# First k and q by head over two queues, a later second part, and last rows in four blocks: sliding-window attention before a gated FFN

## The chip, the cores and the metric

The kernel runs on one core of a Trainium2 chip. The metric is device microseconds of one execution, from the first to the last instruction of the launch. A profile of one execution has a span that is a little shorter than that run's time (323.3 against 324.98 us before the change).

## The reference

Attention with a causal window of 64 tokens, then a feed-forward layer with a ReLU gate. Only shapes and the computation are kept:

```python
B, H, S, D = 8, 8, 576, 64                      # q, k, v: (B, H, S, D) float32
rel = pos[:, None] - pos[None, :]
mask = (rel >= 0) & (rel < 64)
scores = where(mask, q @ k.T / sqrt(D), -1e9)
attn = softmax(scores)                          # per head
x = (attn @ v).transpose(0, 2, 1, 3).reshape(4608, 512)
out = (relu(x @ w_gate) * (x @ w_val)) @ w_out  # w_gate, w_val: (512, 1536), w_out: (1536, 512)
```

## The kernel before

The 4608 rows of x are cut into token tiles: four of 384 and six of 512. Attention works on units of 192 tokens; a unit covers all eight heads, and two units make a tile of 384. With 576 tokens per batch, units 0, 1 and 2 are the tokens 0 to 191, 192 to 383 and 384 to 575 of batch 0. Heads are taken in two halves of four, `hh` 0 for heads 0 to 3 and `hh` 1 for heads 4 to 7; within a half, head g lies in partitions 32g to 32g+31.

k and q come from HBM with 32 runs of tokens per head, one run in each partition, 18 tokens long. A vector-engine transpose of 32x32 blocks (`qk_trans`, L185) turns them to the layout that the score matmuls need. Everything after batch 0's first heads is loaded by GpSimd's DMA queue with a cast to fp16 on the way (`qk_load`, L167). Heads 0 to 3 of batch 0 are different: `first_load` (L172) takes all 576 tokens as fp32 over SP's queue, k and then q, and `first_round` (L178) rounds each to fp16 in two halves, one on the vector engine (DVE) and one on the scalar engine (ACT).

A unit then goes through these steps. `u_st` (L233) makes the scores on TensorE (PE), `u_exp` (L267) their exponentials on ACT, `u_mask` (L272) the mask on DVE (units 0 and 1 have the mask as a bias in the scores instead, `bias_mm`, L210), `u_pv` (L293) the values with a column of row sums, `u_recip` and `u_norm` (L307 to L317) the division, and `u_turn` (L327) transposes the result into the tile's `xt`. `v_load` (L191) brings v by GpSimd's queue, and `v_spread` (L200, L202) copies it to the other partition half, so that a window's 128 keys stand in one column of partitions.

`hidden` (L468) multiplies a tile's `xt` by wg and wv, block by block of the 12 blocks of 128 hidden columns; ACT applies the ReLU (L453) and DVE the gate (L456). `output` (L482) multiplies by wo, ACT copies PSUM to `o_sb` (L489), and SP stores it (L490). `output_last` (L505) treats the last 128 rows of the last tile on its own: two halves of 256 columns, and the second half is evacuated in two parts on two engines.

The weights come by `w_load` (L148, L150), four blocks of columns at a time, each of wg and wv in two transfers (the two halves of the contraction), also over GpSimd's queue and with a cast. They are issued behind k, q and v of the first units, so that the order on this queue is: k and q of heads 4 to 7, v of units 0 and 1, wg and wv 0 to 3, wg and wv 4 to 7, v of unit 2, wg and wv 8 to 11, then batch 1 and wo. `bands` (L100) makes the mask and the identity matrix on GpSimd, behind the first two loads.

The order of instructions on each engine is written out in the program. From the first `hidden` on, a planner (`Weaver`) keeps a modelled clock of PE's work and a heap of pieces with due times: `W.at(26.0, ...)` puts the scores of unit 2 behind the matmul group at which the modelled clock passes 26.0, and so on. The due times decide places in the engines' queues, not moments on the chip. `heat` issues matmuls of zeros ahead of the real work. The tile framework adds the semaphore waits; a DMA's completion is counted on one of eight semaphores in turn for each kind of queue, and a new DMA on a semaphore waits for the one before it there.

Of the kernel before, what the change touches and what calls it, by code (L numbers as in the profile page):

```python
# [10 lines left out]
FP32 = mybir.dt.float32  # L11
FP16 = mybir.dt.float16
# [32 lines left out]
def kernel(  # L45
# [10 lines left out]
    nc = tc.nc  # L56
    B, H, S, D = q.shape
    DM = H * D
# [7 lines left out]
    G = 4  # L66
# [3 lines left out]
    NS = 4  # L70
# [26 lines left out]
    bias = consts.tile([128, 64], FP16)  # L97
    ident = consts.tile([128, 128], FP16)

    def bands():  # L100


        nc.gpsimd.memset(mask, 1.0)
        nc.gpsimd.memset(ident, 1.0)
        for band, lo, hi in ((ident, 0, 0), (mask, 64, -1)):
            n = band.shape[1]
            nc.gpsimd.affine_select(  # L107
                out=band, in_=band, compare_op=mybir.AluOpType.is_ge, fill=0.0,
                base=lo, pattern=[[1, n]], channel_multiplier=-1,
            )  # L110
            nc.gpsimd.affine_select(
                out=band, in_=band, compare_op=mybir.AluOpType.is_ge, fill=0.0,
                base=hi, pattern=[[-1, n]], channel_multiplier=1,
            )

    def band_bias():

# [45 lines left out]
    def qk_load(b, name, hh):  # L163

        tile_ = nat[b, name, hh] = a_in.tile([128, S // 32 * D], FP16, name=f"{name}{hh}", bufs=2)
        src = (q if name == "q" else k)[b, G * hh:G * hh + G]
        nc.gpsimd.dma_start(tile_, src.rearrange("h (i j) d -> (h i) (j d)", i=32))  # L167

    def first_load(name):

        t32 = nat["32", name] = x_sb.tile([128, S // 32 * D], FP32, name=f"{name}32", bufs=1)
        nc.sync.dma_start(t32, (q if name == "q" else k)[0, 0:G].rearrange("h (i j) d -> (h i) (j d)", i=32))  # L172

    def first_round(name, copies):
        n = S // 32 * D // len(copies)
        to = nat[0, name, 0] = a_in.tile([128, S // 32 * D], FP16, name=f"{name}0", bufs=2)
        for i, copy in enumerate(copies):
            copy(to[:, n * i:n * i + n], nat["32", name][:, n * i:n * i + n])  # L178

    def qk_trans(b, name, hh, j0=0, j1=S // 32):  # L180

        src = nat[b, name, hh].bitcast(FP32).rearrange("p (j e) -> p j e", e=32)
        dst = qTs[b % 2][:, hh] if name == "q" else kTs[b % 2][:, hh, 64:64 + S]
        dst = dst.bitcast(FP32).rearrange("p c o -> p (c o)")
        nc.vector.transpose(dst.rearrange("p (i j) -> p j i", i=32)[:, j0:j1], src[:, j0:j1])  # L185
# [8 lines left out]
    def v_spread(u, copy=None, h0=0, h1=H):  # L194

        b, uu = divmod(u, UB)
        t = v16s[b % 2]
        copy = copy or nc.vector.tensor_copy
        for g0, g1 in (((0, 3),), ((4, 5),), ((6, 7),))[uu]:
            copy(t[64:128, g0:g1:2, h0:h1, 0:64], t[0:64, g0 + 1:g1 + 1:2, h0:h1, 0:64])  # L200
        for g0, g1 in (((2, 3),), ((4, 5),), ((6, 9),))[uu]:
            copy(t[0:64, g0:g1:2, h0:h1, 0:64], t[64:128, g0 - 1:g1 - 1:2, h0:h1, 0:64])  # L202
# [73 lines left out]
    def u_pv(u, hhs=(0, 1), banks=None):  # L276

        d = units[u]
        if "pv" not in d:
            if banks:  # L280
                d["pv"] = [one_bank("pv") for _ in range(2)]
            else:
                both = two_banks("pv")
                d["pv"] = [both[:, hh] for hh in range(2)]
                d["both"] = both
        for hh in hhs:
            to = d["pv"][hh]
            for w in range(UB):
                b, vw = divmod(UB * u + w, NG)
                for s in range(2):  # L290
                    for j in range(G):
                        c = VW * (2 * w + s)
                        nc.tensor.matmul(  # L293
                            to[32 * j:32 * j + 32, c:c + D + 1], p_of(u, G * hh + j, w)[:, 32 * s:32 * s + 32],
                            v16s[b % 2][:, vw, G * hh + j, 0:D + 1],
                            start=True, stop=True, skip_group_check=True)
        return 0.27 * len(hhs)
# [185 lines left out]
                         start=(f == 0), stop=(f == NF - 1))  # L483
        W.clock += 519 / 2400.0

    def out_evac(t, op, sub):
        def evac():
            o_sb = f_sb.tile([128, DM], FP32, name="o_sb")
            nc.scalar.copy(o_sb, op)  # L489
            nc.sync.dma_start(out[bass.ds(starts[t] + sub * 128, 128)], o_sb)  # L490
        W.at(W.clock, evac)

    def op_tile():
# [2 lines left out]
    def output(t, subs=None):  # L496
        for sub in range(widths[t] // 128) if subs is None else subs:
            op = op_tile()
            for f in range(NF):
                if f % 4 == 0:  # L500
                    W.advance(W.clock)
                out_mm(t, op, sub, f)
            out_evac(t, op, sub)

    def output_last(t):  # L505

        last = widths[t] // 128 - 1
        output(t, range(last))
        W.drain()
        for col in range(2):  # L510
            op = op_tile()
            for f in range(NF):
                g_sb, _ = gs[t]
                nc.tensor.matmul(op[:, 0:256], g_sb[:, f, bass.ds(last * 128, 128)], wo[:, f, 256 * col:256 * col + 256],
                                 start=(f == 0), stop=(f == NF - 1))
            parts = ((0, 256, nc.scalar.copy, nc.sync),) if col == 0 else (
                (0, 128, nc.scalar.copy, nc.scalar), (128, 256, nc.vector.tensor_copy, nc.sync))
            for c0, c1, copy, queue in parts:
                o_sb = f_sb.tile([128, DM], FP32, name="o_sb")
                copy(o_sb[:, c0:c1], op[:, c0:c1])  # L520
                queue.dma_start(out[bass.ds(starts[t] + last * 128, 128), 256 * col + c0:256 * col + c1], o_sb[:, c0:c1])

    def output_by_rows(t):
        ops = [op_tile() for _ in range(TT // 128)]
# [8 lines left out]
    with tc.manual_schedule():  # L533
        G3, V3, O3 = ([(wt, src, f0, f0 + 4) for f0 in (0, 4, 8)]
                      for wt, src in ((wg, moe_w_gate), (wv, moe_w_val), (wo, moe_w_out)))
        act, dve, pool = nc.scalar.copy, nc.vector.tensor_copy, nc.gpsimd.tensor_copy
        for name in "kq":
            first_load(name)
        for name in "kq":
            qk_load(0, name, 1)  # L540
        warm = consts.tile([128, 2], FP32)
        nc.vector.memset(warm, 0.0)
        nc.scalar.activation(warm[:, 1:2], warm[:, 0:1], ACT.Exp)
# [3 lines left out]
        nc.vector.memset(zero, 0.0)  # L547
        st_tiles(0)
        heat(6, units[0]["st"][3])
        bands()  # L550
        v_load(0, ((1, 0, 128), (3, 0, 64)))
        v_load(1, ((3, 64, 128), (5, 0, 128)))
        w_load(*G3[0], 15.2)
# [1 line left out]
        k_zeros()  # L555
        band_bias()

        first_round("k", (dve, act))
        u_bias(0)
        u_bias(1)  # L560
        qk_trans(0, "k", 0)
        first_round("q", (act, dve))
        qk_trans(0, "q", 0)
        for name in "kq":
            qk_trans(0, name, 1)
        for hh in range(2):
# [4 lines left out]
        for hh in range(2):  # L571
            v_spread(0, dve, G * hh, G * hh + G)
            u_pv(0, (hh,), True)
        v_spread(1, pool)
        for hh in range(2):
            u_recip(0, (hh,))
# [11 lines left out]
        v_load(2)  # L588
        w_load(*G3[2], 27.0)
        w_load(*V3[2], 29.6)  # L590
        W.at(26.0, lambda: u_st(2))
        plan_exps(26.0, 2)
        W.at(25.5, lambda: v_spread(2))
        plan_values(29.5, 2)

        for name in "kq":
            for hh in range(2):
# [106 lines left out]
```

The softmax here doesn't subtract the row's maximum and nothing guards it: scores larger than these inputs give would overflow.

## Time and profile before

| what | value |
|---|---|
| time, median of 3 runs | 324.99 us (324.95 to 325.98) |
| span of the profiled execution | 323.3 us (its run: 324.98) |
| mean granted TensorE clock | 0.989 |
| GpSimd's DMA queue | 18.29 MB written, 48.4% of 16 engines' span |
| SP's DMA queue | 10.55 MB, 8.9% |
| HBM | 37.75 MB read, 9.44 MB written |

The page lists busy times of the engines (PE is TensorE, PEld its weight loads, DVE VectorE, ACT ScalarE, POOL GpSimd, SP the queue of stores), then the chain of work that ended last. In a timeline, each line has the start, the busy time, engine, source line, operation, what it writes and reads, how many instructions are merged in it, and in brackets how long the engine had been idle and what ended that. Names with a q (SPq, ACTq, DVEq) are the engine's sequencer: it issues DMAs and waits for semaphores. Sizes on the page count the type that is written, so a cast load of 256 KB reads 512 KB.

### The profile page before, as it was taken

The numbers are of one execution on the slowest core, as the hardware profiler recorded it, in microseconds if no ns is written. First come the engines' busy times: TensorE is split into PE (matmuls) and PEld (weight loads), VectorE is DVE, ScalarE is ACT, GpSimd is POOL, SyncE is SP. The second block draws the span as 40 slices with busy tenths as digits, with TensorE's granted clock in tenths as the row PEclk, the third lists the DMA queues.
The fourth block names the chain that finished last, engine by engine and source line by source line (L and its number), as shares of the span: only waits on it lengthen the run. The fifth ranks groups of instructions, "written<-read, shape, count | busy, mean of one in ns | idle before, by whom it ended". The sixth has DMA issues, their size and how long they took to land.

```text
span 323.3 us, 8901 instructions
## 1 busy us (share of the span) xinstructions
PE 313.7 (97%) x3851; PEld 168.4 (52%) x3851; DVE 192.1 (59%) x370; ACT 127.0 (39%) x249; POOL 93.7 (29%) x138
## 2 busy tenths in 40 slices
PE   5699999999999999999999999999999999999995
PEld 2586958656556644454445444454445444544443
DVE  5947962687938749564755656674767146723410
ACT  3444324534424523532454234613372237223321
POOL 8766335285900390029000910071000000000000
PEclk9599999999999999999999999999999999999999
DMA  7999998989590269019900892091001200020002
GB/s 215 186 196 210 194 107 174 155 150 163 83 211 4 15 108 181 3 12 124 214 5 2 111 203 24 2 122 70 0 2 38 97 0 2 21 111 3 0 34 98
DMA packets 52488, 29.48 MB, mean 91 GB/s; under 512 B 38880, under 2 KB 43872, under 8 KB 52448
## 3 DMA queue, kind: packets, MB, share of 16 engines
q0 software_dynamic: 46688, 18.29, 48.4%
q1 hardware_dynamic: 5616, 10.55, 8.9%
q8 instruction: 30, 0.49, 0.6%
q10 hardware_dynamic: 144, 0.07, 0.1%
q14 instruction: 10, 0.08, 0.1%
HBM read 37.75 MB, written 9.44 MB: 146 GB/s over the span
## 4 chain that ended last, share of the span: by engine, by line
PE 94%; DMA 2%; POOL 2%; issue 0%; ACT 0%; DVE 0%; DVEq 0%; POOLq 0%
PE h L468 59%; PE op L482 28%; PE st L233 3%; PE pv L371 2%; DMA v<-in_v_dram 2%; PE pv L293 1%; POOL v L191 1%; DMA out_dram<-o_sb 1%; POOL k L167 0%; POOL v L200 0%; POOL v L202 0%; ACT o_sb L489 0%; POOL q L167 0%; PE st L207 0%; POOL ident L107 0%
## 5 line engine op out<-in xcount | busy, mean ns | idle before, releaser
L456 DVE TENSOR_TENSOR g_sb<-r_sb,h 128x512 f16<-128x512 f32 (+1 forms) x120 | 75.4, 631 | 86.3 <-PE h L468 84.5
L468 PE MATMUL h<-xt,wg 128*128 128x512 f16 (+2 forms) x544 | 112.5, 338 | 0.1
L468 PE MATMUL h<-xt,wv 128*128 128x512 f16 (+2 forms) x544 | 111.3, 335 | 0.0
L453 ACT ACTIVATE r_sb<-h 128x512 f32<-128x512 f32 (+1 forms) x120 | 66.7, 558 | 89.5 <-PE h L468 80.4
L482 PE MATMUL op<-wo,g_sb 128*128 128x512 f16 x420 | 93.9, 379 | 0.0
L468 PEld LDWEIGHTS <-wg 128*128 128x128 f16 x544 | 51.5, 99 | 42.8 <-issue 0.5
L468 PEld LDWEIGHTS <-wv 128*128 128x128 f16 x544 | 50.5, 98 | 40.8
L482 PEld LDWEIGHTS <-g_sb 128*128 128x128 f16 x420 | 40.3, 98 | 47.1
L191 POOL DMA_DIRECT2D v<-in_v_dram x41 | 34.5, 861 | 95.0 <-PE pv L371 90.1
L489 ACT COPY o_sb<-op 128x512 f32<-128x512 f32 x35 | 20.5, 586 | 84.7 <-PE op L482 84.5
L356 DVE TENSOR_TENSOR pw<-pw,mask 128x512 f16<-128x512 f16 x48 | 19.3, 422 | 14.6 <-ACT pw L352 14.3
L352 ACT ACTIVATE pw<-st 128x512 f16<-128x512 f32 x48 | 25.7, 605 | 5.0 <-PE st L233 4.5
L200 POOL COPY v<-v 64x512 f16<-64x512 f16 (+1 forms) x21 | 15.5, 736 | 24.3 <-DMA v<-in_v_dram 23.4
L185 DVE STREAM_TRANSPOSE kT<-k 128x576 f32<-128x576 f32 x16 | 19.9, 1245 | 0.2 <-ACT k L178 0.2
L185 DVE STREAM_TRANSPOSE qT<-q 128x576 f32<-128x576 f32 x16 | 19.3, 1237 | 0.1
L267 ACT ACTIVATE p<-st 128x384 f16<-128x384 f32 (+1 forms) x40 | 14.0, 441 | 8.2 <-PE st L233 8.2
L391 DVE TENSOR_TENSOR xw<-pv,rw 128x448 f16<-128x448 f32 (+1 forms) x36 | 16.2, 507 | 0.4
L233 PE MATMUL st<-qT,kT 32*128 32x64 f16 x1152 | 12.9, 192 | 3.5 <-DVE qT L185 3.5
L202 POOL COPY v<-v 64x512 f16<-64x512 f16 (+1 forms) x21 | 15.9, 759 | 1.0
L233 PEld LDWEIGHTS <-kT 32*128 32x128 f16 x1152 | 10.8, 94 | 10.5 <-issue 8.5
L396 DVE STREAM_TRANSPOSE xt<-xw 128x1024 f16<-128x1024 f16 x12 | 14.9, 1244 | 0.4
L272 DVE TENSOR_TENSOR p<-p,mask 128x384 f16<-128x384 f16 x24 | 9.5, 414 | 3.6 <-ACT p L267 3.5
(46 smaller groups left out, 97.9 us busy)
## 6 DMA issues: line engine op xcount, KB each, us to landing
out_dram<-o_sb SPq DMA_DIRECT2D x35, 256.0 KB, 2.8
k<-in_k_dram POOLq DMA_DIRECT2D x15, 288.0 KB, 5.7
q<-in_q_dram POOLq DMA_DIRECT2D x15, 288.0 KB, 8.6
v<-in_v_dram POOLq DMA_DIRECT2D x31, 128.0 KB, 8.9
wg<-in_moe_w_gate_dram POOLq DMA_DIRECT2D x6, 256.0 KB, 6.4
wv<-in_moe_w_val_dram POOLq DMA_DIRECT2D x6, 256.0 KB, 7.7
wo<-in_moe_w_out_dram POOLq DMA_DIRECT2D x3, 512.0 KB, 12.2
v<-in_v_dram POOLq DMA_DIRECT2D x10, 64.0 KB, 5.8
```

What stands on the lines that cost most here:

```text
L185: nc.vector.transpose(dst.rearrange("p (i j) -> p j i", i=32)[:, j0:j1], src[:, j0:j1])
L191: nc.gpsimd.dma_start(v16s[b % 2][lo:hi, g, :, 0:64], v[b, :, 64 * g - 64 + lo:64 * g - 64 + hi].rearrange("h p d -> p h d"))
L202: copy(t[0:64, g0:g1:2, h0:h1, 0:64], t[64:128, g0 - 1:g1 - 1:2, h0:h1, 0:64])
L233: return [lambda dh=dh: nc.tensor.matmul(to, kTs[b % 2][rows, hh, 64 * w:64 * w + 128, dh], qTs[b % 2][rows, hh, 64 * w:64 * w + 64, dh], ...
L352: nc.scalar.activation(d["p"][g].rearrange("p n c -> p (n c)"), d["st"][g], ACT.Exp, scale=scale)
L356: nc.vector.tensor_tensor(p, p, mask[:, None, :].to_broadcast([128, 2 * QW, 64]), MUL)
L391: nc.vector.tensor_tensor(d["x"][:, hh, s0:s1], pv[:, :, 0:D].rearrange("p s (c e) -> p s e c", e=2), d["r"][:, hh, s0:s1, :, None].to_bro ...
L453: nc.scalar.activation(part(r_sb), part(h1), ACT.Relu)
L456: nc.vector.tensor_tensor(g_sb[:, f:f + w, c0:c0 + n], part(r_sb), part(h2), MUL)
L468: nc.tensor.matmul(h[:, b * n:b * n + n], wt[:, c, (f + b) * 128:(f + b) * 128 + 128], xt[:, c, c0:c0 + n], start=(c == 0), stop=(c == NC ...
L482: nc.tensor.matmul(op, g_sb[:, f, bass.ds(sub * 128, 128)], wo[:, f], start=(f == 0), stop=(f == NF - 1))
L489: nc.scalar.copy(o_sb, op)
```

## The change

Four things change together.

First, k and q of heads 0 to 3 of batch 0 are loaded in two parts: tokens 0 to 383, which units 0 and 1 use, and tokens 384 to 575, which only unit 2 uses. The first part of k goes out over SP's queue and that of q over ACT's queue, each as four transfers, one for each head (32 partitions). The second parts go over SP's queue; a one-column memset of their tiles on DVE, placed behind the v copies of unit 0, holds them back until then. Rounding and transposing are split in the same way, and the second part's is planned at due times 22.4 to 23.6.

Second, GpSimd makes the mask ahead of the load of k of heads 4 to 7, and the identity between that and the load of q.

Third, the due times of unit 2's work are 0.5 earlier.

Fourth, the last 128 rows are made in four blocks of 128 columns, each with its own tile, copied by ACT; three are stored by SP and the last one by ACT. The first rows of the last tile are stored in two transfers.

```diff
-        for band, lo, hi in ((ident, 0, 0), (mask, 64, -1)):
...
+    def band(to, lo, hi):
+        nc.gpsimd.memset(to, 1.0)
...
-        nc.sync.dma_start(t32, (q if name == "q" else k)[0, 0:G].rearrange("h (i j) d -> (h i) (j d)", i=32))
...
+    def part_load(queue, name, t0, t1):
+        src = q if name == "q" else k
+        for g in range(G):
+            queue.dma_start(parts[name, t0][32 * g:32 * g + 32], src[0, g, t0:t1].rearrange("(i j) d -> i (j d)", i=32))
+
+    def part_round(name, t0, t1, copies):
...
+        for i, copy in enumerate(copies):
+            copy(to[:, c0 + n * i:c0 + n * i + n], parts[name, t0][:, n * i:n * i + n])
+
+    def part_trans(name, t0, t1):
+        src = nat[0, name, 0][:, t0 // 32 * D:t1 // 32 * D].bitcast(FP32).rearrange("p (j e) -> p j e", e=32)
...
+        nc.vector.transpose(dst.rearrange("p (i j) -> p j i", i=32), src)
...
-        for col in range(2):
+        for c0, c1, queue in ((0, 128, nc.sync), (128, 256, nc.sync), (256, 384, nc.sync), (384, DM, nc.scalar)):
             op = op_tile()
             for f in range(NF):
                 g_sb, _ = gs[t]
-                nc.tensor.matmul(op[:, 0:256], g_sb[:, f, bass.ds(last * 128, 128)], wo[:, f, 256 * col:256 * col + 256],
+                nc.tensor.matmul(op[:, 0:c1 - c0], g_sb[:, f, bass.ds(last * 128, 128)], wo[:, f, c0:c1],
                                  start=(f == 0), stop=(f == NF - 1))
...
+            o_sb = consts.tile([128, c1 - c0], FP32, name=f"o_last{c0}")
+            nc.scalar.copy(o_sb, op[:, 0:c1 - c0])
+            queue.dma_start(out[bass.ds(starts[t] + last * 128, 128), c0:c1], o_sb)
...
-        for name in "kq":
-            first_load(name)
-        for name in "kq":
-            qk_load(0, name, 1)
+        for name, queue in (("k", nc.sync), ("q", nc.scalar)):
+            for t0, t1 in ((0, TT), (TT, S)):
+                part_tile(name, t0, t1)
+            part_load(queue, name, 0, TT)
+        band(mask, 64, -1)
+        qk_load(0, "k", 1)
+        band(ident, 0, 0)
+        qk_load(0, "q", 1)
...
         for hh in range(2):
             v_spread(0, dve, G * hh, G * hh + G)
             u_pv(0, (hh,), True)
+        for name in "kq":
+            nc.vector.memset(parts[name, TT][:, 0:1], 0.0)
+            part_load(nc.sync, name, TT, S)
         v_spread(1, pool)
...
-        W.at(26.0, lambda: u_st(2))
-        plan_exps(26.0, 2)
-        W.at(25.5, lambda: v_spread(2))
-        plan_values(29.5, 2)
+        for i, name in enumerate("kq"):
+            W.at(22.4 + 0.6 * i, lambda name=name: part_round(name, TT, S, (act,)))
+            W.at(23.0 + 0.6 * i, lambda name=name: part_trans(name, TT, S))
+        W.at(25.5, lambda: u_st(2))
+        plan_exps(25.5, 2)
+        W.at(25.0, lambda: v_spread(2))
+        plan_values(29.0, 2)
```

## The prediction

> **What bounds the kernel now.** I read the page first (busy shares, then the chain that ended last), then the chain in order of time, then the timelines of the vector engine, of PE and of GpSimd for the first 30 us, then the stage table, and last the timeline of the end.
>
> ```profile
> PE 313.7 (97%) x3851; PEld 168.4 (52%) x3851; DVE 192.1 (59%) x370; ACT 127.0 (39%) x249; POOL 93.7 (29%) x138
> ...
> PE 94%; DMA 2%; POOL 2%; issue 0%; ACT 0%; DVE 0%; DVEq 0%; POOLq 0%
> ```
>
> TensorE carries 94% of the chain. What else can be won is at the two ends. The chain in order of time shows the first:
>
> ```profile
> 4.08 2.21 POOL v L191 x3
> 6.29 5.55 DMA v<-in_v_dram
> ...
> 11.99 0.64 POOL v L200
> ...
> 14.67 2.25 PE h L468 x15
> 16.93 0.10 issue
> 17.03 9.48 PE h L468 x81
> ```
>
> From 17.03 PE runs without a gap to 317.28. So the time is the moment of that line plus a fixed amount of PE work plus the tail. What holds 17.03 is the transposed x of unit 1, and the vector engine makes that in an almost unbroken row:
>
> ```profile
> 4.89 0.46 DVE L178 CAST k<-k 128x576 f16<-128x576 f32 x1 [0.59 <-DMA k<-in_k_dram]
> 5.59 1.26 DVE L185 STREAM_TRANSPOSE kT<-k 128x576 f32<-128x576 f32 x1 [0.24 <-ACT k L178]
> 6.70 0.80 DVE L178 CAST q<-q 128x576 f16<-128x576 f32 x1
> 7.60 1.26 DVE L185 STREAM_TRANSPOSE qT<-q 128x576 f32<-128x576 f32 x1
> 8.70 1.24 DVE L185 STREAM_TRANSPOSE kT<-k 128x576 f32<-128x576 f32 x1
> 9.78 1.23 DVE L185 STREAM_TRANSPOSE qT<-q 128x576 f32<-128x576 f32 x1
> ...
> 16.27 1.03 DVE L327 STREAM_TRANSPOSE xt<-x 128x384 f16<-128x384 f16 x2
> ```
>
> It starts when k has landed (4.89) and idles only 0.6 us until 17.3, so an earlier or shorter start moves 17.03. Below it lies a second limit. The DMA engines are full from 2 us on (the stage table has a share of 1.0 or more in each microsecond from 3 to 18), and the weights are queued behind k, q and v. GpSimd's waits show when they land:
>
> ```profile
> 23.47 0.54 POOL L167 DMA_DIRECT2D k<-in_k_dram  x1 [1.70 <-DMA wv<-in_moe_w_val_dram]
> ...
> 26.86 0.92 POOL L191 DMA_DIRECT2D v<-in_v_dram  x1 [0.52 <-DMA wg<-in_moe_w_gate_dram]
> ```
>
> The second half of wv's columns 4 to 7 was issued at 15.33 and took 7.9 us: landed 23.2. That of wg's columns 8 to 11 was issued at 18.27 and took 8.3: landed 26.6. PE starts these groups at 23.74 and 26.92 and reaches the second half two 128x384 matmuls (0.33 us at 16 in 2.65) later: needed at 24.07 and 27.25. The slack is 0.87 and 0.68 us. PE can't move ahead by more than that unless the weights do.
>
> The end, from the timeline:
>
> ```profile
> 319.97 0.27 ACT L520 COPY o_sb<-op 128x128 f32<-128x128 f32 x1 [0.94 <-PE op L514]
> 320.26 0.37 ACTq L521 DMA_DIRECT2D out_dram<-o_sb  x1
> 320.34 0.29 DVE L520 COPY o_sb<-op 128x128 f32<-128x128 f32 x1 [10.05 <-ACT o_sb L520]
> ```
>
> PE is done by 319.9. The vector engine's copy of the last 128 columns starts only at 320.34: the chain has the 2.01 us transfer of an older o_sb (317.91 to 319.92) and then four 0.05 us semaphore steps before it. Its transfer leaves at 320.66 and takes 1.7 us: 322.33, and the span closes 0.97 later, at 323.3.
>
> [...] The new loads go to 32 partitions each, and both queues walk the heads in one order[...]. The trace of before has no such load. [...] k is issued in 0.38 us, q in 0.42, and they take 4.1 and 5.0 to land. [...]
>
> **The change, part by part.**
>
> *First loads.* 2 x 576 KB of k and q in row on SP become 2 x 384 KB, k on SP and q on ACT, four transfers each. At 0.35 to 0.4 us an issue the fourth leaves near 2.2 on both queues. On ACT they stand ahead of the 1.28 us table load, which then ends near 3.7, plus 0.2 for the warm exp: 3.9, before any data lands, so free. Data began at about 1.6. The stage table's 336 to 383 GB/s from 2 to 5 us is the upper rate[...]. 786 KB (10^3 bytes) takes 2.1 or 3.6 us; with 0.3 to 0.5 for ramp and landing, both have landed at 4.3 (full rate) or at 5.7 to 6.1 (half). I take the second, 5.9.
>
> *Casts and transposes.* Cast halves shrink from 576 to 384 elements: DVE 0.46 to about 0.33, ACT 0.67 to 0.49 (the row of r_sb 128x384 has that). Transposes fall from 1.26 to 2/3, 0.83 each. From landing L: ACT's half L+0.5, k's transpose L+0.55 to L+1.38, q's cast to L+1.65, q's transpose L+1.7 to L+2.53. Before: 8.86. With L=5.9: 8.43, a gain of 0.43. With L=4.3 it is 6.83, but then heads 4 to 7 hold the row (next). With 6.1, 0.2.
>
> *GpSimd's order.* The mask (0.19+0.24+0.24 and gaps, 0.75) now precedes k of heads 4 to 7, the identity (0.8) precedes q's. Both transfers issue 0.75 and 1.5 later; the sum is the same, so the v loads still start at 4.0. Their transposes at 8.70 and 9.78 waited for no transfer; k and q landed at 7.7 and 9.2 (issue plus time to landing: 1.31+6.4, 2.00+7.2). With 393 KB less ahead of them, or the same time at half rate, they land no later than about 9.2, and q's transpose starts at 9.5 or 8.9. So the row's gain is 0.4, or 0.9 in the full-rate case.
>
> *Vector engine's two memsets* (0.06 each, row of the 128x2 memset) fall in its 0.40 us wait for the first values: nothing. Behind them on SP queue eight loads of 48 KB, about 0.4 each to issue, from near 11.8 to 15. Nothing else is on SP until 48.8.
>
> *The rest's bytes.* 393 KB leave the stretch ahead of v and enter among the weights: by the time wv's first half is in, the same bytes have passed. At 400 GB/s of reads (a 512 KB weight half each 1.28 us) that is 0.98 us out and 0.98 in: zero, except for what the first loads lose to half rate. That is 3.6-2.1 = 1.5, less the ramp that before wastes anyway (0.4: 60 GB/s in the second microsecond), less what GpSimd's transfers fill in meanwhile, 0.4 to 1.0. Weights come 0.1 to 0.7 late; I take 0.4. Then PE may move by 0.68-0.4 = 0.28. In the full-rate case they come on time: 0.68.
>
> *Late rounding.* Two ACT copies (0.49) and two transposes of 192 columns (0.42 each) come between relus and gates near 23 to 25. The rounds end near 24.6 and the transposes at 25.05, ahead of the scores at 26.4; ACT and DVE idle 2.6 and 2.7 us around there. DVE's gates, v spread and masks then end about 0.3 to 0.5 later, at 29.0, just in time for the values of unit 2 (29.6 less the gain). Between 0 and 0.2; I take 0. The planned times that move by 0.5 leave PE's order as it was.
>
> *Tail.* Four blocks of 12 matmuls at N=128: 48 x 56 = 2.69 us, against 24 x 109 = 2.62. Each copy (0.27) fits in the next block (0.67). The last block is copied at 320.0, its transfer leaves ACT at 320.3 and lands 1.6 later, 321.9; the three on SP leave earlier. The DVE copy with its waits is gone: 322.33 to 321.9, -0.45. [...] Splitting one older store costs SP 0.33, hidden.
>
> **Sum.** Head -0.28, tail -0.45: -0.7. The profiled span is 323.3 and its run 324.98; the others were 324.95, 324.99 and 325.98. So 324.99-0.7 = 324.3.
>
> **Rivals.** (1) The first loads run at full rate. For: two queues could fill the slow start (60 GB/s before 2 us). Head -0.68 to -0.85, tail -0.45: 323.7. (2) The rest's loads get in the weights' way, at half rate, with 1.5 us or more: PE waits for wg's columns 8 to 11, and the head loses 0.3 to 1.0: 324.8 to 325.5. It decides from 0.68 us of delay on; above 1.13 the whole is slower than before. Against: SP issues them spread over 3 us, and cast weights write only half of what they read. (3) Weight loads set the pace at N=128[...]. The point is a pace over 65 ns (48 x 9 = 0.45). Against: 40 ns per row group at N=64 with 128-column loads in the scores (48 in 0.48 us, four groups). (4) The granted clock, 0.5 from 9.8 to 16.8[...]; earlier PE work at half clock can cost 0.1 to 0.3.
>
> **How the numbers follow.** Half-rate case 0.48 (own range 323.9 to 324.7), full rate 0.33 (323.3 to 324.0), weights late 0.11, N=128 slow 0.08. The measurement tells about 0.3%, 0.97 us, from no change. Faster by that (under 324.02): 0.31 of the full-rate case and 0.07 of the half-rate one, 0.38. Slower by it (over 325.96): half of the slow-tail case, and late weights worse than priced, 0.08. Range 323.4 to 325.3.
>
> **What would show it.** k's and q's first casts at 5.6 to 6.1 (half rate) or 4.3 to 4.6 (full); the first long h row at 16.6 or 16.2 in place of 17.03, with or without a gap near 26.5 for wg; N=128 blocks of 0.67 us; the last landing at 321.9 less the head's gain. An h row after 17.03, a wait of PE for weights of over 0.7[...] would prove it wrong.

## The result and the profile after

The changed kernel takes 326.94 us (median of 6 runs, 326.01 to 327.19) against 325.00 us for the kernel before on the same chip: a ratio of 1.0048, interval 1.0031 to 1.0065. It is slower by about 1.6 us by the ratio (1.9 by the medians), where the forecast was 0.7 faster, and it lies above the range. The profiled execution has a span of 325.5 us (its run: 327.19, the longest of the six) against 323.3, so the two traces to compare differ by 2.2. Its mean granted TensorE clock is 0.984 (0.989 before). Three of the six executions had 0.984 and took 326.93 to 327.19; the others, at 0.989 and 0.990, took 326.01, 326.32 and 326.94.

The page first, with the lines that answer to those shown of before:

```profile
PE 314.9 (97%) x3875; PEld 169.7 (52%) x3875; DVE 192.0 (59%) x373; ACT 127.6 (39%) x253; POOL 93.6 (29%) x138
...
PE 94%; DVE 2%; DMA 2%; issue 1%; SPq 0%; ACT 0%; DVEq 0%; ACTq 0%
```

PE is still 94% of the chain and its work has grown by 1.2 us only. What is new is in the small shares: DVE had 0% of the chain and has 2%, and the DMA share now belongs to another transfer. The chain in order of time (start, us, what) names it:

```profile
2.18 5.98 DMA k<-in_k_dram
...
8.26 0.52 ACT k L182
...
10.80 1.08 DVE kT L195
...
12.99 0.67 DVE v L210
13.66 0.03 issue
13.69 0.57 DVE v L212
...
16.87 12.30 PE h L478 x96
```

Before, the chain came through v, from GpSimd's queue. Now it starts with the fourth of the four loads of k: issued on SP at 2.18, landed at 8.16. From there it runs through the vector engine's row without leaving it, until PE's long row of `hidden`. The vector engine's timeline has the same row:

```profile
8.28 0.36 DVE L182 CAST k<-k 128x384 f16<-128x384 f32 x1 [5.68 <-DMA k<-in_k_dram]
8.81 0.85 DVE L188 STREAM_TRANSPOSE kT<-k 128x384 f32<-128x384 f32 x1 [0.16 <-ACT k L182]
9.51 0.34 DVE L182 CAST q<-q 128x384 f16<-128x384 f32 x1
9.95 0.85 DVE L188 STREAM_TRANSPOSE qT<-q 128x384 f32<-128x384 f32 x1
...
18.47 1.03 DVE L337 STREAM_TRANSPOSE xt<-x 128x384 f16<-128x384 f16 x2
```

The first cast starts at 8.28, where it started at 4.89 before: 3.39 later, after an idle time of 5.68 that ended with the arrival of k. The casts and transposes are as short as they were meant to be. The x of unit 1 is ready at 19.50 instead of 17.30.

The stage table shows the transfers themselves (columns: stretch, us, then busy time of PE, PEld, DVE, ACT and POOL, the granted clock, the DMA engines' share, GB/s). Before:

```profile
2.00:3.00 1.00, 0.65 (x2) 0.28 (x3) 0.57 (x4) 0.29 (x2) 0.92 (x5) 1.00 0.84 336
3.00:4.00 1.00, 1.00 (x3) 0.30 (x2) 0.00 (x0) 0.00 (x0) 0.86 (x4) 1.00 1.01 355
4.00:5.00 1.00, 1.00 (x4) 0.42 (x3) 0.29 (x2) 0.11 (x1) 1.00 (x3) 1.00 0.99 383
```

After:

```profile
2.00:3.00 1.00, 0.65 (x2) 0.28 (x3) 0.60 (x5) 0.32 (x1) 0.86 (x4) 1.00 0.89 283
3.00:4.00 1.00, 1.00 (x3) 0.29 (x2) 0.00 (x0) 0.99 (x2) 1.00 (x3) 1.00 0.85 142
4.00:5.00 1.00, 1.00 (x4) 0.41 (x3) 0.00 (x0) 0.18 (x1) 1.00 (x2) 1.00 0.98 193
```

The DMA engines are nearly as busy as before, but in the fourth and fifth microsecond they move 142 and 193 GB/s instead of 355 and 383. The eight loads were issued from 0.81 to 2.21 on the two queues. The first pair of each landed early (k at 3.62 and 4.21, q at 3.86 and 4.63), the second pair only at 7.14 and 8.16, and at 7.31 and 8.33. GpSimd's load of k of heads 4 to 7, issued at 1.52 between the second and the third, landed at 8.54.

The way from there to the span can be added up. The row starts 3.39 late; shorter casts and transposes give 1.45 back (first cast to end of q's transpose 2.52 us, 3.97 before), which leaves 1.94. DVE's first two copies of v take 0.67 and 0.57 instead of 0.29 and 0.22, while GpSimd's two copies of v run at the same time (12.91 to 14.18); that costs 0.73, and the 0.40 us wait for the first values that stood there before is gone. At the end of x the lag is 2.20. PE's row of wg takes 4.46 instead of 3.99, since the granted clock is at half until 20.27 (16.42 before): the lag is 2.66 at the row of wv (21.16 against 18.50), and PE keeps it to the last blocks. The end gives 0.5 back: 2.2. The profiled execution is one of the three with the lower clock, so the 0.46 of this last step need not be in the other three.

At the end PE's last four blocks and the last store look like this:

```profile
319.80 2.84 PE L525 MATMUL op<-wo,g_sb 128*128 128x128 f16 x48
...
322.68 0.27 ACT L528 COPY o_last<-op 128x128 f32<-128x128 f32 x1 [0.41 <-PE op L525]
322.97 0.38 ACTq L529 DMA_DIRECT2D out_dram<-o_last  x1
```

The 48 matmuls end at 322.65 in the chain, the last copy follows at once, its store leaves ACT at 322.97 and lands at 324.58: 1.94 after PE, where it was 2.44 after PE (319.89 to 322.33). DVE has no part in it any more. The span closes 0.92 after the landing, as before. (The spans are 325.50 and 323.25 to the hundredth; the forecast's 0.97 came from the rounded 323.3.)

### The profile page after: what moved, and what is told of

It is laid out like the page before. It is cut to its first block, busy times and chain, and to the rows that moved or that the text cites. A ratio compares the mean times of both kernels' runs of the same rounds, so it can differ in the third digit from the quotient of the medians.

```text
span 325.5 us, 8983 instructions
## 1 busy us (share of the span) xinstructions
PE 314.9 (97%) x3875; PEld 169.7 (52%) x3875; DVE 192.0 (59%) x373; ACT 127.6 (39%) x253; POOL 93.6 (29%) x138
## 4 chain that ended last, share of the span: by engine, by line
PE 94%; DVE 2%; DMA 2%; issue 1%; SPq 0%; ACT 0%; DVEq 0%; ACTq 0%
PE h L478 59%; PE op L492 28%; PE st L243 3%; PE pv L381 2%; DMA k<-in_k_dram 2%; PE pv L303 1%; PE op L525 1%; SPq L175 0%; DVE x L327 0%; DVE kT L195 0%; DVE v L210 0%; DVE qT L188 0%; DVE v L212 0%; ACT k L182 0%; DVE xt L337 0%
## 5 line engine op out<-in xcount | busy, mean ns | idle before, releaser
L195 DVE STREAM_TRANSPOSE kT<-k 128x576 f32<-128x576 f32 x15 | 18.7, 1245 | 0.0
L195 DVE STREAM_TRANSPOSE qT<-q 128x576 f32<-128x576 f32 x15 | 18.1, 1238 | 0.0
L212 POOL COPY v<-v 64x512 f16<-64x512 f16 (+1 forms) x21 | 15.9, 759 | 1.0
```

## The experiments

My first theory was the forecast's own, called ports in the expectations: loads into 32 partitions at a time go at half the rate. This was an assumption; the trace of before has no such load and does not show it. The rivals were that the pieces lose their place behind GpSimd's load, and that small transfers are slow whatever their shape.

**Only the last rows.** The kernel before with the changed end and its split store, nothing else.

```diff
-        for col in range(2):
+        for c0, c1, queue in ((0, 128, nc.sync), (128, 256, nc.sync), (256, 384, nc.sync), (384, DM, nc.scalar)):
```

> The kernel before with only the last part of the change (last rows in four blocks of 128 columns, older store in two). Theory of the whole study: all of the loss comes from the head, so this alone is faster by 0.45 us, 324.5, and the last transfer is issued near 320.3 with no vector-engine copy behind it. Rival, that weight loads set the pace at N=128[...].

Measured: 325.34 us (14 runs, 324.94 to 326.02) against 325.14, ratio 1.0002 (0.9988 to 1.0015). The tail alone shows no gain. In its profile PE ends at 320.53 and the last store lands at 322.46, so the landing is 0.5 earlier relative to PE, as priced. But the span closes 1.71 after the landing, not 0.92.

**k and q of the kernel before as four transfers each, by head and by columns.** All 576 tokens, all on SP. By head each transfer writes 32 partitions; by columns each writes a quarter of the row of all 128 partitions.

```diff
-        nc.sync.dma_start(t32, (q if name == "q" else k)[0, 0:G].rearrange(...))
+        for g in range(G):
+            nc.sync.dma_start(t32[32 * g:32 * g + 32], (q if name == "q" else k)[0, g].rearrange("(i j) d -> i (j d)", i=32))
```

By columns, the two new lines are:

```diff
+        for c in range(0, S // 32 * D, 288):
+            nc.sync.dma_start(t32[:, c:c + 288], (q if name == "q" else k)[0, 0:G].rearrange(...)[:, c:c + 288])
```

> The kernel before with its two first loads (576 tokens, SP's queue) cut by head into four transfers of 32 partitions each. Ports theory[...]: k lands at 4.9 to 5.5, q not before 7.5. Count theory (each of many small transfers has its own cost at its end): k at 6 or later, q at 8 or later. If neither holds: 4.9 and 6.2 as before.

> The kernel before with its two first loads cut by columns into four transfers each, all of 128 partitions: the same number of transfers as by head[...]. Ports theory: k at 4.9 and q at 6.2 as before. Count theory: as late as by head, k at 6 or later and q at 8 or later.

Measured: 329.39 by head and 330.22 by columns (one run each; the kernel before 325.14). By head the last of k landed at 7.91 and of q at 11.18; by columns at 9.42 and 11.62; in one transfer each they land at 4.87 and 6.24. Both fall in the count theory's expectation. The pieces that write all partitions are no better than those that write 32, and all four last landings are 3.0 to 5.4 us late. That speaks against the ports theory, but does not settle it: by columns a packet has 1152 bytes (1024 data packets for 1.18 MB) instead of the 4608 of before, and short packets are a rival here. Both also have the order of arrival in common. By head the first two pieces of k were in at 3.46 and 4.16, the last two at 5.50 and 7.91, with GpSimd's load at 6.23 between them; by columns two pieces of k, issued ahead of GpSimd's load at 1.31, were in by 3.51, that load itself came at 7.33, and the pieces issued behind it at 7.51 and 9.42.

**Two queues alone.** The kernel before, with q's single transfer of 576 tokens on ACT's queue.

```diff
+        queue = nc.scalar if name == "q" else nc.sync
-        nc.sync.dma_start(t32, ...)
+        queue.dma_start(t32, ...)
```

> The kernel before with q's first load on ACT's queue, everything else the same: one transfer of 128 partitions on each of two queues. If two hardware queues at once are the cost: both land at 7 or later. If not: both land near 6.0 to 6.3, k later than its 4.87 of before, and the time is 0.3 to 1.0 us longer, since the vector engine's row starts with k. Theory of sharing with GpSimd's queue: they land a little later than 6.3[...].

Measured: 326.22 us (20 runs), ratio 1.0034 (1.0024 to 1.0044). k landed at 6.22 and q at 6.39. Both end about when q ended before (6.24), and k, which the vector engine needs first, is 1.35 later. Here two queues at once made the first of two transfers later and the second no earlier. The time is 1.1 us longer by the ratio, a little over the 0.3 to 1.0 expected.

**q's heads in the order 2, 3, 0, 1.** The changed kernel; at each moment k and q then write different halves of the partitions.

```diff
-        for g in range(G):
+        for g in (2, 3, 0, 1) if queue is nc.scalar else range(G):
```

> The changed kernel with q's first four transfers in the order of heads 2, 3, 0, 1, so that at each moment the two queues write to different halves of the partitions. Ports theory: first k and q all landed by 5.5 to 6.3 in place of 8.2 to 8.3. Count theory and theory of sharing with GpSimd's queue: no change, 8.0 to 8.5.

Measured: 326.37 us (one run); last of k at 7.67, of q at 7.84. That is 0.5 of the 3.4, between the two expectations, and as much as any run here assigns to the ports theory. The transfers' rates say the same. In slices of 0.3 us, the changed kernel moved 389 and 359 GB/s from 2.4 to 3.0, when the pieces of heads 0 and 1 were on their way, all of them in partitions 0 to 63; the forecast's full rate was 336 to 383, from the trace of before. Then it moved 195, 123, 118 and 113 until 4.2. With q's heads in the other order it moved 379 and 410 from 2.4 to 3.0, and 141, 84, 123 and 133 from 3.3 to 4.5. So the slow stretch is hardly a matter of which half of the partitions is written.

**GpSimd's loads held back.** The changed kernel; two one-column copies on GpSimd, which read all 128 partitions, make its first load wait until all of k and q have landed (issue at 7.34).

```diff
+        if b == 0 and name == "k":
+            nc.gpsimd.tensor_copy(tile_[:, 0:1], parts["k", 0][:, 0:1])
+            nc.gpsimd.tensor_copy(tile_[:, 1:2], parts["q", 0][:, 0:1])
```

> The changed kernel with GpSimd's loads held back until the first k and q have landed (two one-column copies on GpSimd into the tile of k of heads 4 to 7, overwritten by the load). Theory of sharing: alone on the engines the first loads land by 4.5 to 5.0. Ports theory: 5.6 to 6.1. Count theory: still 7 or later. The time is not of interest here: v and the weights start late.

Measured: k landed at 3.66, 4.35, 5.86 and 6.39, q at 3.94, 4.66, 6.03 and 6.56. The last is 1.8 earlier than in the changed kernel, so GpSimd's load does get in front of the later pieces. But 6.4 is still not 4.9, and none of the three expectations held: another part is in the pieces themselves. The slow stretch is there without GpSimd's load, 166 GB/s from 3 to 4 us with the engines' share at 1.10 (142 at 0.85 in the changed kernel). (The time, 329.6 us, says nothing: v and the weights come later too.)

**Mask and identity both ahead of GpSimd's first load.** The changed kernel; the load is issued at 2.43 instead of 1.52, behind the issue of all eight pieces.

```diff
         band(mask, 64, -1)
-        qk_load(0, "k", 1)
         band(ident, 0, 0)
+        qk_load(0, "k", 1)
         qk_load(0, "q", 1)
```

> The changed kernel with GpSimd making both the mask and the identity ahead of its first load, so that this is issued at about 2.7 us, after the last of the eight first transfers (2.2), and not between them. Theory of issue order: the first k and q are all landed by 6.4 to 6.8, the vector engine's row starts 1.5 to 1.8 us earlier than in the changed kernel, and the time falls to about 325.3. Theory of mere sharing by turns: 7.3 to 8.0, and 326.3 or more.

Measured: 325.62 us (12 runs, 324.92 to 326.44), ratio 1.0017 (1.0008 to 1.0025); last of k at 7.27, of q at 7.45, first cast at 7.39. One line of order takes back 1.0 us by the two ratios (0.0031 of 325). The landings are at the early edge of the second expectation (7.3 to 8.0), the time is between the two: even a load that is issued behind all pieces delays them (7.27 and 7.45, against 6.39 and 6.56 with the load held back).

**One transfer each.** The changed kernel with the first part of k and of q in one transfer of 128 partitions, 12 of each partition's 18 tokens: the same bytes, though the tokens of heads 0 to 3 aren't the reference's.

```diff
+        if t0 == 0:
+            queue.dma_start(parts[name, t0], src[0, 0:G].rearrange("h (i j) d -> (h i) (j d)", i=32)[:, 0:t1 // 32 * D])
-        for g in range(G):
+        for g in range(G) if t0 else ():
```

> The changed kernel with the first part of k and of q as one transfer of 128 partitions each, the same 384 KB on the same two queues. It takes the first 12 tokens of each partition's 18, so the tokens of heads 0 to 3 are not the reference's; all else, with the second parts by head, stays. Theory of the number of transfers: k and q land by 4.6 to 5.2, the vector engine's row starts there, the first long row of h comes at 16.2 to 16.6, and with the tail the time is 323.8 to 324.3. Theory that two queues or GpSimd are the cost: 6 or later and 325 or more.

Measured: k landed at 4.75 and q at 4.95, with GpSimd's load again issued at 1.52. The fourth microsecond of the stage table moves 387 GB/s instead of 142:

```profile
3.00:4.00 1.00, 1.00 (x3) 0.30 (x2) 0.00 (x0) 0.00 (x0) 1.00 (x3) 1.00 0.98 387
```

So the cut into pieces is the cause: two queues, the bytes and GpSimd's order are the changed kernel's, and 3.4 us of delay are gone. One thing besides the number differs, since each transfer now writes 128 partitions and not 32; the run with the other order of heads and the rates beside it speak against that. GpSimd's load, though issued at the same time, moved its first bytes at 4.25, when the last of k was through; in the changed kernel they came at 3.75, among the pieces. The vector engine's timeline:

```profile
4.77 0.36 DVE L184 CAST k<-k 128x384 f16<-128x384 f32 x1 [2.17 <-DMA k<-in_k_dram]
5.31 0.85 DVE L190 STREAM_TRANSPOSE kT<-k 128x384 f32<-128x384 f32 x1 [0.18 <-ACT k L184]
...
10.12 0.29 DVE L212 COPY v<-v 64x512 f16<-64x512 f16 x1 [0.58 <-DMA v<-in_v_dram]
```

But the time was 325.22 us (12 runs), ratio 1.0002 (0.9994 to 1.0011), and not the 323.8 to 324.3 expected. PE's timeline shows where the head's gain went:

```profile
13.49 4.00 PE L480 MATMUL h<-xt,wg 128*128 128x192 f16 x32
...
27.12 2.45 PE L480 MATMUL h<-xt,wg 128*128 128x384 f16 x14 [0.38 <-DMA wg<-in_moe_w_gate_dram]
29.50 0.56 PE L305 MATMUL pv<-v,p 128*32 128x65 f16 x48
```

PE starts on wg 1.18 earlier than before (14.67), but its matmuls of wv's columns 8 to 11 start at 29.99 where they started at 30.11. Of the 1.06 lost, 0.38 is a wait for wg, and another 0.52 is in the three rows ahead of it, which take 2.90, 3.06 and 2.88 instead of 2.80, 2.76 and 2.76. In the last two of them the time is a wait for weights as well, too short for the list: the second halves landed at 20.63 and 23.34, and PE goes on at 20.67 and 23.39. This is the second limit that the forecast had named. The second half of wg's columns 8 to 11 landed at 27.08, 0.51 later than before, and PE's gain of 1.18 shrank to 0.12; the forecast's slack of 0.68 less these 0.51 would be 0.17.

**The end again.** The 1.71 us of the first experiment needed a cause. At the end SP waits for the eight DMA semaphores one after the other. Before, the last store counted on the eighth; with two more stores it counted on the second, and six more waits came behind it. (40 loads and stores of SP and ACT before, five on each semaphore; 42 with the changed end.) Two kernels test this, both from the kernel before: three blocks of 256, 128 and 128 columns without the split store, and the changed end with two rows of tile 5 stored in four pieces each, which moves the last store on by six (the turn, below). The diffs are against the first experiment.

```diff
-((0, 128, nc.sync), (128, 256, nc.sync), (256, 384, nc.sync), (384, DM, nc.scalar))
+((0, 256, nc.sync), (256, 384, nc.sync), (384, DM, nc.scalar))
```

> The kernel before with a last part in three blocks (256 and 128 columns stored by SP, 128 by ACT), each with its own tile and ACT's copy, and no older store cut: as many stores as before, so that the last one uses the eighth of the eight completion semaphores again. Theory of the order of the final waits: the last landing is 0.45 to 0.5 us nearer to the end of PE's work and the span closes 0.9 to 1.0 after it, so 0.4 to 0.5 us faster than before, 324.5. Rival, that the tail's gain was never there (time of the first tail run): same as before, 325.0.

```diff
-            out_evac(t, op, sub, (0, 256, DM) if sub == 0 and t == NS + NL - 1 else (0, DM))
+            out_evac(t, op, sub, (0, 256, DM) if sub == 0 and t == NS + NL - 1 else (0, 128, 256, 384, DM) if sub < 2 and t == 5 else (0, DM))
```

> The first tail run (four blocks) with two stores of an earlier tile cut in four, six stores more, which turns the semaphore of the last store from the second of the eight to the eighth and leaves the tail as it is. Theory of the order of the final waits: the span closes 0.9 to 1.0 us after the last landing in place of 1.7, and the time is 0.4 to 0.5 us under that of before. Rival: more transfers, same or slower than the first tail run.

Measured: 324.68 us (21 runs), ratio 0.9992 (0.9985 to 0.9999), and 324.85 us (13 runs), ratio 0.9991 (0.9983 to 0.9999). The span closes 0.92 and 0.91 after the last landing. SP's semaphore waits stand in the packed traces, one behind the other:

| kernel | last store counts on | ends of SP's waits, us after the last landing | span closes, us after it |
|---|---|---|---|
| before | eighth | 0.04 | 0.92 |
| changed end, with the turn | eighth | 0.04 | 0.91 |
| changed end alone | second | 0.04, 0.11, 0.55, 0.63, 0.70, 0.77, 0.83 | 1.71 |
| one transfer each (above) | second | 0.05, 0.11, 0.17, 0.23, 0.29, 0.35, 0.42 | 1.27 |

From the end of the last wait to the end of the span it is 0.86 to 0.88 in all four. So six more waits cost 0.37; the first experiment's profile has another 0.4 between two of them, and what held SP there is not shown. The ratios of the changed end without and with the turn differ by the same 0.36 us, though their intervals overlap. Both kernels gain 0.3, a little under the 0.4 to 0.5 expected. Of the kernels that leave nothing out these are the two fastest; both are just clear of the kernel before by their intervals, and 1.8 us faster than the changed one by the ratios.

**One transfer each with the right tokens, and without the second parts.** The heads are a dimension of their own in the source; two rows of tile 5 are stored in pieces for the turn. The second kernel leaves the second parts' loads out.

```diff
-        for g in range(G):
-            queue.dma_start(parts[name, t0][32 * g:32 * g + 32], src[0, g, t0:t1].rearrange("(i j) d -> i (j d)", i=32))
+        queue.dma_start(parts[name, t0], src[0, 0:G, t0:t1].rearrange("h (i j) d -> h i (j d)", i=32))
```

> The changed kernel with each part of k and q of heads 0 to 3 in one transfer for all four heads (128 partitions, the right tokens), and two rows of tile 5 stored in four and in two pieces, so that the last store falls on the eighth semaphore. If the number of transfers made the first loads late and the turn of the last store's semaphore took back the tail's gain: first casts at 4.6 to 5.0, the last landing 1.9 to 2.0 after PE's end, the span closing 0.9 after that, and a median of 324.4 to 324.8, 0.4 under the kernel with one transfer each alone (325.2), with the weights still holding PE near 27 (a wait for wg of 0.2 to 0.6). Rival, the second parts in single transfers get a larger share of the DMA engines than in eight small ones: weights 0.3 to 0.6 later, a median of 324.8 to 325.3.

> The kernel before this one, with the second parts (tokens 384 to 575 of heads 0 to 3, k and q) not loaded at all but zero, so unit 2's scores of heads 0 to 3 aren't the reference's; 393 KB are missing from between v and the weights. If the weights hold PE in the head: all weights land 0.8 to 1.1 earlier (wg's columns 8 to 11 at 26.0 to 26.3 for 27.1), PE has no wait for them, its matmuls of wv's columns 8 to 11 start at 29.0 to 29.4 in place of 30.0, and the median is 323.7 to 324.1. Rival, the granted clock's half-rate windows or the vector engine hold it: the weights come earlier, but those matmuls start at 29.8 to 30.1 and the median is within 0.2 of the other kernel's.

Measured: 334.88 us (5 runs), ratio 1.0306 (1.0289 to 1.0323), and 335.46 us (4 runs), 1.0322 (1.0307 to 1.0336). Neither expectation held. The first cast:

```profile
15.90 0.36 DVE L181 CAST k<-k 128x384 f16<-128x384 f32 x1 [13.30 <-DMA k<-in_k_dram]
```

It is 11 us later than with one transfer of 128 partitions. The list of DMA queues for the first 20 us shows what differs (packets, MB, share of 16 engines). This kernel, ACT's queue, which carries q alone:

```profile
q10 hardware_dynamic: 132, 0.39, 5.8%
```

The kernel with one transfer each:

```profile
q10 hardware_dynamic: 144, 0.39, 5.3%
```

The changed kernel, four transfers:

```profile
q10 hardware_dynamic: 192, 0.39, 6.9%
```

Each has 128 data packets, one for each partition. What is over is 16 for one transfer and 64 for four, so 16 for each (in the trace of the changed kernel, 64 packets of 4 bytes beside 128 of 3072); here it is 4. The outermost dimension of this transfer is the four heads; of the other two it is the partitions, 128 and 32. That the dimension makes it slow fits the 4, but the profile does not show why, and the expectation had not looked at it. These two kernels so tell nothing on the second parts, but their end agrees with the turn: the first one's last landing is at 332.25, its span 333.17. The right 384 tokens in one transfer with another outermost dimension weren't tried.

**The last question again.** One transfer each as above (the one of 128 partitions) with the turn, with and without the second parts.

```diff
-        for name in "kq":
-            nc.vector.memset(parts[name, TT][:, 0:1], 0.0)
-            part_load(nc.sync, name, TT, S)
```

> The changed kernel with the first part of k and of q in one transfer of 128 partitions each (same bytes; the tokens of heads 0 to 3 aren't the reference's), and two rows of tile 5 stored in four pieces each, so that the last store falls on the eighth semaphore. If that turn costs 0.35: the span closes 0.9 to 0.95 after the last landing, and the median is 324.7 to 324.9 (325.2 without the turn). Rival, the turn is not what the end waits for: closing 1.3, and 325.2.

> The kernel e15 without the loads of the second parts (tokens 384 to 575 of heads 0 to 3 are zero, so unit 2's result isn't the reference's either); 393 KB are missing from between v and the weights. The eight fewer transfers leave the turn as it is. If the weights hold PE in the head: wg's columns 8 to 11 are in at 26.0 to 26.4 in place of 27.1, PE does not wait for them, its matmuls of wv's columns 8 to 11 start at 29.0 to 29.5 in place of 30.0, and the median is 0.4 to 0.9 under e15. If the granted clock or the vector engine holds it: those matmuls start at 29.8 to 30.1 and the median is within 0.2 of e15.

Measured: with them 325.03 us (14 runs, 324.47 to 325.51), ratio 0.9991 (0.9983 to 0.9999); without them 324.37 us (22 runs, 323.5 to 325.74), ratio 0.9980 (0.9972 to 0.9988). In the first the span closes 0.92 after the landing, 1.27 without the turn, as expected. The medians with and without the turn come from two chips and differ by 0.2; the ratios differ by 0.0011, that is 0.36 us, the price of the six waits, but no more than their intervals. Leaving the second parts out gives 0.66 by the medians and 0.36 by the ratios: within or just under the expectation for weights that hold PE. The profiled executions do not show that mechanism, though. In both, wg's columns 8 to 11 landed at 26.7 to 26.8 (26.0 to 26.4 was expected without the second parts), and PE did not wait for them, because it was late for another reason:

```profile
14.07 5.18 PE L480 MATMUL h<-xt,wg 128*128 128x192 f16 x32
```

That is the kernel with the second parts. The granted clock was at half until 18.97, and this row took 1.19 longer than the 3.99 of before. Without them it was 4.83 from 14.73 on, with half clock until 18.91; this profiled execution, 325.55 us, is one of the slowest of the 22.

The times by clock say more. Without the second parts 13 of the 22 executions had a mean granted clock of 0.995 or more; with them none of the 14 had. At 0.988 and 0.989 the medians are 324.83 and 325.03, only 0.2 apart, while the 13 have a median of 324.2. In the kernel before, the higher clock alone is worth little: eight of its executions on these chips at 0.994 or 0.995 took 324.90 to 325.13, with a median of 324.95 against 325.03. So more than half of the 0.66 goes with the clock, and why it was higher without these loads is not shown.

## Why the prediction was wrong, step by step

**First loads.** This is the step that failed. The text: "With 0.3 to 0.5 for ramp and landing, both have landed at 4.3 (full rate) or at 5.7 to 6.1 (half). I take the second, 5.9." They landed at 8.16 and 8.33. (The sum is also a little off as written: from the text's start at 1.6 it gives 4.0 to 4.2 and 5.5 to 5.7. The first bytes of before came at 1.83, which gives 5.7 to 5.9.) It priced eight transfers as so many bytes at a rate, and both ends of the bound were rates. The full rate was read from the stage table of before; the half rate (3.6 us for 786 KB) was an assumption that no trace shows. What the runs showed: one transfer of 128 partitions for each, over the same two queues with the same GpSimd load behind them, lands at 4.75 and 4.95, nearer the full-rate end. Made into four by head, the same bytes take 3.4 us longer. The cost is in the cut into pieces, which had no term but the sequencer's 0.4 an issue. It splits into about 1.8 for GpSimd's load, which enters between pieces that are issued 0.45 apart, and 1.6 for the pieces themselves (6.56 with that load held back against 4.95). For the mechanism of that 1.6 the traces have only the symptom: from the third pieces on, the engines are busy (a share of 1.10 from 3 to 4 us with GpSimd held back) and move 166 GB/s. That the last piece is issued 1.4 us after the first can be part of it, though the engines were busy meanwhile. The mechanism stays open.

No case of the range had the first loads later than 6.1. Rival 2 had the sign, by another way: late weights, for which PE never waited here.

**The half rate.** The assumption that loads into 32 partitions at a time go at half the rate was the reason for 5.9. The traces do not bear it out as the bound here: 389 GB/s went into one half of the partitions from 2.4 to 2.7, with k and q in different halves 0.5 was gained, and pieces over all 128 partitions, in shorter packets, were no faster. A share of 0.5 remains possible. That both queues walk the heads in one order was the right observation with the wrong weight.

**GpSimd's order.** "With 393 KB less ahead of them, or the same time at half rate, they land no later than about 9.2." They landed at 8.54 and 9.99, and q's transpose of those heads had its place in the row only at 11.72, so they were in time. The issue was off: 1.52 and 3.10, so 0.21 and 1.10 later than before and not 0.75 and 1.5, because the mask ran from 0.81 on, when GpSimd had stood idle before. And the step looked at what GpSimd's load waits for, and not at who waits behind it; issued at 1.52 rather than 2.43 it cost 1.0 us.

**Casts and transposes.** Right: 0.36 and 0.34 for 0.33, 0.85 for 0.83, and 2.52 from the first cast to the end of q's transpose for 2.53 (2.64 from k's landing).

**Behind the row.** Two terms were not in the sum. DVE's copies of v met GpSimd's in time (0.73, less the 0.40 wait). In the trace the copies are slow only where the two overlap: 0.67 and 0.57 from 12.99 on, 0.29 and 0.24 from 14.29 on, with GpSimd's from 12.91 to 14.18. And in this execution the half clock lasted from 10.03 to 20.27: 0.46. Rival 4 had 0.1 to 0.3 for it, from a stretch that it read as 9.8 to 16.8 (the trace of before has 9.59 to 16.42).

**The rest's bytes and late rounding.** Nothing of it can be seen in the changed kernel: with PE 2.66 late it waits for no weights. So the 0.28 was never tested there. In the kernel with one transfer each the second limit did what the forecast said it would: the weights were 0.51 late (0.4 in the forecast, 0.1 to 0.7), and 1.18 us earlier at the first wg row became 0.12 (0.28 in the forecast). The full-rate rival's head gain of 0.68 to 0.85 was therefore too large as well. The second parts' share in this is 0.66 by the medians, 0.2 of it at equal clock; what the rest is made of I could not settle, since the profiled executions of these two kernels had half clock until 18.97 and 18.91.

**Tail.** The parts were right: 48 matmuls in 2.69 as worked out, the DVE copy with its waits gone, the landing 0.5 earlier for 0.45. The 56 ns of the forecast agree with the trace of before: its matmuls start 82 to 83 ns apart at N=192 and 109 to 110 at N=256, and a straight line through both gives 56 at N=128, as an estimate. In the changed kernel they start 55 to 56 ns apart, so the slower pace of rival 3, for which no trace gave a figure, did not come. There the gain reached the span (the closing took 0.92), and that was luck: with 16 loads and 40 stores, 56 in all, the last store again counted on the eighth semaphore, as with the 40 of before. "Splitting one older store costs SP 0.33, hidden" is right for its time, but the number of DMAs also decides on which of eight semaphores the last store counts, and that is worth 0.37 at the end for six waits (0.8 in one profile). In the kernel before with only this tail it took the gain back. The forecast had the closing as a constant.

**What would prove it wrong.** "An h row after 17.03" was named. The changed kernel's chain has its long row at 16.87, but that is the start of the whole row, which was at 14.67 before; the matmuls of wv behind it went from 18.50 to 21.16.

## What to carry to other kernels

In these runs a transfer that the chain waits for was best left whole. Ahead of cutting one, count the pieces, the time between their issues and what other queues issue in between, and only then the bytes. Look at the outermost dimension of the DMA pattern too: here, with the four heads there, k's cast began at 15.90 instead of 4.77. Move later loads behind the urgent ones by their issue, on whichever queue they are. Before pricing a gain in the head, find the next limit behind the first one (here weights and clock: 1.2 us became 0.1); before pricing one in the tail, look at what the program does between its last store's landing and its end.

## What the runs showed of the hardware that was not expected

- The same 393 KB of k and of q landed at 4.75 and 4.95 in one transfer each, at 8.16 and 8.33 in four each by head, and at 15.9 for k in one transfer whose outermost dimension is the four heads.
- A load on one queue, issued between pieces on two others, came in among them: held back, it let the last piece land at 6.56 instead of 8.33; issued 0.9 later, at 7.45.
- Two transfers of 590 KB on two queues at once landed at 6.22 and 6.39; one after the other on one queue, at 4.87 and 6.24.
- At the end of these programs SP waits for eight DMA semaphores one after the other (321.09 to 322.37 before). The span closed 0.91 or 0.92 us after the last landing when the last store counted on the eighth (before, the changed kernel, and those with the turn), and 1.27 and 1.71 after it on the second.
- The granted clock was at half from 9.59 to 16.42 us before, from 10.03 to 20.27 in the changed kernel, and until 15.95 in the kernel with one transfer each, 18.97 in that with the turn and 18.91 in that without the second parts: stretches of 6.83 us, and one of 10.24. Where the stretch lies matters: with its end at 16.42 PE's first wg row took 3.99, with its end at 18.97 it took 5.18, both stretches 6.83 long. These 1.2 us are more than most of the differences that this study measures.
